# Attention and mixture kernel on one core: softmax sums divided out of the attention output, zero-padded rows in the third score term, one step order

## The chip, the core and the metric

The kernel runs on one core of a Trainium2 chip. The core has five engines with instruction queues of their own: TensorE (PE; its weight loads are shown apart as PEld), VectorE (DVE), ScalarE (ACT), GpSimd (POOL) and SyncE (SP), which here issues every DMA. Engines meet only at semaphores. The metric is device time in microseconds (us) for one launch; lower is better. Three runs of the kernel before took 892.65, 895.05 and 895.09 us, a median of 895.05 us.

## The reference

Three layers run in a row, all results in float32.

```
q, k, v: 4 batches, 12 heads, 448 rows, head size 64
rmsnorm(x, g) = x / sqrt(mean(x*x) + 1e-6) * g
attn = softmax(rmsnorm(q, g_q) @ rmsnorm(k, g_k).T / 8)      # e / (sum(e) + 1e-9)
x = heads side by side of attn @ v                           # 1792 x 768
g = x @ w_gate;  val = x @ w_val                             # 768 x 1536 each
h = g * sigmoid(g) * val;   x2 = h @ w_out                   # 1536 x 768
logits = x2 @ phi                                            # 32 slots, 4 for each of 8 experts
dispatch = softmax over tokens, combine = softmax over slots
slot_out[e] = relu((dispatch.T @ x2)[e] @ w1[e]) @ w2[e]     # 768 -> 1024 -> 768
out = combine @ slot_out                                     # 1792 x 768
```

w_gate, w_val and w_out arrive as float64 words.

## The kernel before

**Steps.** Two heads of one batch are a pair; there are 24 pairs, six a batch. A pair has four blocks of 112 queries, so c = 0 to 3 counts the steps of a pair, and `t` counts the 96 attention steps. From step 28 on each step also does one unit `u` of 128 columns of gate or value (`gv`, L573): 18 matmuls in two halves, G0 and G1. Even units are gate, odd ones value; 24 units make a batch, 96 make all four. A step of one batch's gate and value therefore goes beside the attention of the batch that follows.

**Order.** All of it stands in `tc.manual_schedule()`: each engine executes its instructions in the order in which the Python code issues them. A step is a dictionary of small functions, and a list of their names says in which order they are called. `ORD0` (L1200) is for steps 0 to 27 (`step0`), `ORD1` for the first batch's gate and value, `ORD2` for the next two batches, `ORD3` for the last.

**Attention of a pair.** q and k are squared (ACT), summed (DVE), turned into inverse roots (POOL, L336 and L337) and multiplied in (POOL, L343). PE transposes them (T, L368). Each is then split into a high part (TH, ACT) and a low part (L, DVE), since a product in the fast float32 format keeps fewer bits; a score is high*high + high*low + low*high. From pair 7 on a stationary tile `qa` holds, for one head, 64 rows of high parts and 64 of low parts of q, and `ka` two copies of k's high parts, so one 128-row matmul gives two terms (L458). The third term, q high by k low (`kl`), is a matmul of 64 rows for each head (L460). Then per head: row maximum (M0, M1; DVE, L465), exponential with its row sum (E0, E1; ACT, L473).

**Dividing by the sums.** `normp` (L478) adds 1e-9 to the two sums of a step (L483), takes reciprocals (L485) and multiplies both heads' 112x448 probabilities in place (L493), all on DVE, one step later. After that PE transposes the probabilities (P0, P1, L503; two steps behind the scores), and V0, V1 (L517) copy them out of PSUM. `pv` (X, L531) multiplies with v; `pv_evac` splits the result into high and low parts `xh`, `xl` for gate and value.

**Weights.** A block of float64 words is made float32 in three moves: two `w_relu` (POOL, L197, R), which give a positive part `hpos` and a negative part `hneg`; `w_top` (POOL, L203), which subtracts one from the other; `w_conv` (DVE, L208, C), which adds the low bits. There is one `hneg` buffer and two `hpos` buffers. Twelve blocks of w_out come in steps 0 to 23, twenty-four of gate and value beside the first batch; later batches read the float32 copy back from DRAM. Each unit's weight is split by `w_hi` (ACT, WH) and `w_lo` (DVE, WL, L235).

**PSUM.** One tag of three buffers (`pt_tile`, L67) serves all transposes, `xp`, the slot logits and the rest in turn; the scores have banks of their own.

**After the steps.** The last part streams the experts' weights from HBM, as buffers come free.

Of the kernel before, what the change touches and what calls it, by code (L numbers as in the profile page):

```python
# [21 lines left out]
def attn_moe_softmoe_kernel(  # L22
# [15 lines left out]
    nc = tc.nc  # L38
# [15 lines left out]
    PRB, PTB = 6, 2  # L54
# [24 lines left out]
    early = tc.alloc_tile_pool(name="early", bufs=1, side="left")  # up to the last batch  # L79
# [90 lines left out]
    def w_load(u):  # L170
        """w_out block u - or, from NO on, gate / value block u - NO."""
# [14 lines left out]
    def w_relu(u, js=(0, 1)):  # L186
        hp, hn = hset[u % 2]
        top = wst[u]["r64"][:, 4 : 4 + 4 * DM].rearrange("p (n w) -> p n w", w=4)[:, :, 0]
        for j in js:
# [5 lines left out]
            else:  # L195
                # what is below zero becomes zero as it is written
# [26 lines left out]
    def w_hi(u):  # L223
        # the last batch has two of them, and its low parts take the place of what they come from
# [13 lines left out]
    def wp_trans(f, hf):  # L238
        """half of w_out block f, transposed."""
# [12 lines left out]
    def wp_mul(f):  # L252
        """w_out @ phi with the slots on the partitions, as sums over four groups of rows of phi."""
# [29 lines left out]
    def load(i, what):  # L283
# [9 lines left out]
        else:  # L293
            vt = ap_.tile([CP, 2, NC, HD], F32, tag="vt", name="vt", bufs=3)
# [8 lines left out]
    def norm_sq(i, ns=(0, 1)):  # L303
        """squares of q and k."""
# [25 lines left out]
    def norm_rs(i, ns=(0, 1)):  # L330
        """one over the root of the mean squares."""
# [7 lines left out]
    def norm_mul(i, n, eng):  # L339
        """q or k over the root of its rows' mean squares, pairs of heads side by side."""  # L340
# [34 lines left out]

    def qk_tiles(i):
        d = st[i]
        if "qa" not in d:
            d["qa"] = ap_.tile([P, 2, S], F32R, tag="qa", name="qa", bufs=2)
            d["ka"] = ap_.tile([P, 2, S], F32R, tag="ka", name="ka", bufs=2)  # L380
            d["kl"] = ap_.tile([P, S], F32R, tag="kl", name="kl", bufs=2)
# [22 lines left out]
    def transp_lo(i, n):  # L404
        """low parts: of q beside the high parts of its head, under a second copy of which k's high parts are."""
# [4 lines left out]
        if i < SPL:  # L410
# [9 lines left out]
            else:  # L420
                sub_lo(kl, tq[:, :S], ka[:, 0])
            return
        for j, r in enumerate(halves):
# [10 lines left out]
            else:  # L434
                sub_lo(kl[r], tq[r, :S], ka[r, j])
# [4 lines left out]
    def scores(t):  # L440
        """scores of a block of queries of two heads; PE."""
# [10 lines left out]
        if i < SPL:  # L452
            for n, (wt, mv) in enumerate(((qa[:, 0], ka[:, 0]), (qa[:, 0], kl), (qa[:, 1], ka[:, 0]))):
# [7 lines left out]
        d[c] = {"sc": sc, "sm": ap_.tile([CP, 4], F32, tag="sm", name="sm", bufs=4), "pr": {}}  # L461

    def smax(t, j):
        d = st[t // NC][t % NC]
        nc.vector.tensor_reduce(  # L465
            out=d["sm"][:, 2 + j : 3 + j], in_=d["sc"][j], axis=AX.X, op=ALU.max, negate=True
        )

    def sexp(t, j):
        d = st[t // NC][t % NC]  # L470
        sm = d["sm"]
        p = ap_.tile([CP, S], F32, tag="pr", name="pr", bufs=PRB)
        nc.scalar.activation(  # L473
            out=p, in_=d["sc"][j], func=AF.Exp, bias=sm[:, 2 + j : 3 + j], accum_out=sm[:, j : j + 1]
# [3 lines left out]
    def normp(t, part=None):  # L478
        """probabilities over their sums."""
        d = st[t // NC][t % NC]  # L480
        pr, sm = d["pr"], d["sm"]
        if part in (0, None):
            nc.vector.tensor_scalar(out=sm[:, :2], in0=sm[:, :2], scalar1=EPS_SUM, scalar2=None, op0=ALU.add)  # L483
        if part in (1, None):
            nc.vector.reciprocal(out=sm[:, :2], in_=sm[:, :2])  # L485
        for j in range(2):
            if part in (2 + j, None):
                if (NP0 if t < M0 else NP1)[t % 2][j] == "p":
                    nc.gpsimd.tensor_scalar(
                        out=pr[j], in0=pr[j], scalar1=sm[:, j : j + 1], scalar2=1.0, op0=ALU.mult, op1=ALU.mult  # L490
                    )
                else:
# [934 lines left out]
```

## Time and profile before

| | us |
|---|---|
| median of three runs | 895.05 (892.65 to 895.09) |
| profiled execution, first to last instruction | 891.2 |
| PE busy | 813.3 (91%) |
| DVE busy | 615.8 (69%) |
| ACT busy | 469.1 (53%) |
| POOL busy | 329.0 (37%) |

The page gives the profiled execution as its span of 891.2 us; the runs' times are 1.4 to 3.9 us above that. Busy shares over the whole span mix parts of different kinds, so the rows below are read by stretches. An idle time is put down to the instruction whose end released it. A float32 matmul of attention output (`xp`) counts as two instructions in the trace.

### The profile page before, as it was taken

Reading aid. Unit: us, or ns where it says so; the run is one execution under the profiler, and the core shown is the slowest. Engines: PE = TensorE matmul, PEld = TensorE weight load, DVE = VectorE, ACT = ScalarE, POOL = GpSimd, SP = SyncE. Lnnn points to the kernel's source line nnn. Section 1 sums busy time; section 2 is a strip of 40 time slices with the busy share of each in tenths; the row PEclk is TensorE's granted clock in tenths of the full one; section 3 lists DMA queues with packets and bytes.
Section 4 is the critical chain, followed back from the end, with each engine's and each line's share of the span. In section 5 each row is a group of like instructions: output and inputs, shape, how many; then the busy total and the mean of one; then the engine's idle time right before and its main releaser. Section 6 shows DMA issues by size and latency. Waiting matters only on the chain.

```text
span 891.2 us, 14391 instructions
## 1 busy us (share of the span) xinstructions
PE 813.3 (91%) x5464; PEld 591.6 (66%) x5464; DVE 615.8 (69%) x1073; ACT 469.1 (53%) x1005; POOL 329.0 (37%) x234
## 2 busy tenths in 40 slices
PE   6888976988988999999999999999999999988675
PEld 6544544766766667777778767787787888745343
DVE  5999999999999996777777777776534443321012
ACT  4767765465556566666667656765532333311012
POOL 8997788877877932032211322120000000001000
PEclk9999999899999999999999999999999999999988
DMA  6645355545645442222232212221214887899997
GB/s 214 191 139 180 114 183 180 168 145 175 189 146 165 141 156 85 82 78 64 86 102 85 77 62 85 64 82 56 65 41 159 284 292 284 326 333 404 402 358 239
DMA packets 77891, 148.87 MB, mean 167 GB/s; under 512 B 5888, under 2 KB 48128, under 8 KB 77824
## 3 DMA queue, kind: packets, MB, share of 16 engines
q1 hardware_dynamic: 77824, 147.97, 50.4%
q8 instruction: 43, 0.70, 0.3%
q14 instruction: 24, 0.20, 0.1%
HBM read 128.29 MB, written 19.66 MB: 166 GB/s over the span
## 4 chain that ended last, share of the span: by engine, by line
PE 61%; DVE 26%; DMA 8%; issue 3%; ACT 1%; POOL 1%; SPq 0%; ACTq 0%; POOLq 0%; DVEq 0%
PE pg L584 33%; DVE pr L493 6%; DMA w<-in_moe_w_dram 5%; PE tp L503 5%; PE xp L531 5%; DVE sm L465 4%; DVE sm L483 4%; DVE raw L208 3%; PE s L458 2%; PE s L460 2%; PE th L619 2%; DVE wl L235 2%; PE lp L640 1%; PE sp L707 1%; DVE ss L323 1%
## 5 line engine op out<-in xcount | busy, mean ns | idle before, releaser
L584 PE MATMUL pg<-xh,wh 128*128 128x448 f32 x576 | 226.7, 394 | 0.0
L584 PE MATMUL pg<-xl,wh 128*128 128x448 f32 x576 | 212.3, 369 | 0.0
L473 ACT ACTIVATE pr<-s,sm 112x448 f32<-112x448 f32 x192 | 121.7, 636 | 91.3 <-DVE sm L465 87.7
L584 PE MATMUL pg<-xh,wl 128*128 128x448 f32 x432 | 159.7, 370 | 0.0
L465 DVE TENSOR_REDUCE sm<-s 112x1 f32<-112x448 f32 x192 | 116.3, 617 | 39.1 <-PE s L460 36.4
L517 ACT COPY pt<-tp 112x448 f32<-112x448 f32 x185 | 98.8, 534 | 74.6 <-PE tp L503 72.8
L493 DVE TENSOR_SCALAR pr<-pr,sm 112x448 f32<-112x448 f32 x192 | 133.3, 716 | 1.4
L503 PE MATMUL tp<-ident,pr 112*112 112x112 f32 x768 | 110.3, 269 | 23.7 <-DVE pr L493 15.3
L584 PEld LDWEIGHTS pg<-xh,wh 128*128 128x128 f32 x576 | 110.0, 191 | 21.5 <-issue 14.1
L503 PEld LDWEIGHTS tp<-ident,pr 112*112 112x112 f32 x768 | 82.0, 137 | 62.4 <-issue 19.6
L584 PEld LDWEIGHTS pg<-xl,wh 128*128 128x128 f32 x576 | 110.2, 191 | 6.5
L336 POOL TENSOR_SCALAR ss<-ss 112x16 f32<-112x16 f32 (+1 forms) x25 | 15.2, 608 | 245.7 <-DVE ss L323 232.0
L227 ACT CAST wh<-raw 128x768 fp32r<-128x768 f32 x96 | 79.8, 832 | 35.9 <-PE pg L584 29.3
L584 PEld LDWEIGHTS pg<-xh,wl 128*128 128x128 f32 x432 | 82.6, 191 | 7.0
L203 POOL TENSOR_TENSOR hpos<-hpos,hneg 128x768 f32<-128x768 f32 x36 | 78.4, 2177 | 3.0
L337 POOL TENSOR_TENSOR ri<-ss,mhalf 112x16 f32<-112x16 f32 (+1 forms) x25 | 72.1, 2884 | 2.1
L235 DVE TENSOR_TENSOR wl<-raw,wh 128x768 fp32r<-128x768 f32 x70 | 69.2, 988 | 0.7
L483 DVE TENSOR_SCALAR sm<-sm 112x2 f32<-112x2 f32 x96 | 53.2, 555 | 11.6 <-ACT pr L473 11.6
L599 DVE SCALAR_TENSOR_TENSOR ht<-ht,pg 128x448 f32<-128x448 f32 x48 | 29.5, 615 | 42.8 <-ACT ht L598 42.7
L531 PE MATMUL xp<-pt,vt 112*64 112x448 f32 x288 | 58.1, 545 | 0.0
L197 POOL TENSOR_SCALAR hneg<-r 128x768 uint16<-128x768 uint16 x36 | 54.5, 1514 | 2.7
L343 POOL TENSOR_TENSOR qn<-qk,ri 112x512 f32<-112x512 f32 x46 | 53.2, 1167 | 1.3
(155 smaller groups left out, 1181.2 us busy)
## 6 DMA issues: line engine op xcount, KB each, us to landing
w<-in_moe_w_dram SPq DMA_DIRECT2D x25, 1536.0 KB, 10.3
raw<-w SPq DMA_DIRECT2D x72, 384.0 KB, 3.2
w<-raw SPq DMA_DIRECT2D x36, 384.0 KB, 5.7
r<-in_moe_w_out_dram SPq DMA_DIRECT2D x12, 768.0 KB, 5.5
r<-in_moe_w_gate_dram SPq DMA_DIRECT2D x12, 768.0 KB, 5.2
r<-in_moe_w_val_dram SPq DMA_DIRECT2D x12, 768.0 KB, 5.2
qk<-in_q_dram SPq DMA_DIRECT2D x24, 224.0 KB, 4.2
qk<-in_k_dram SPq DMA_DIRECT2D x24, 224.0 KB, 4.7
```

The source lines that it names most:

```text
L203: nc.gpsimd.tensor_tensor(out=hp, in0=hp, in1=hn, op=ALU.subtract)
L227: (nc.vector.tensor_copy if u - NO < NU and WH1 == "v" else nc.scalar.copy)(out=wh, in_=wst[u]["raw"])
L235: eng.tensor_tensor(out=wl, in0=wst[u]["raw"], in1=wst[u]["wh"].bitcast(F32), op=ALU.subtract)
L337: nc.gpsimd.tensor_tensor(out=ri, in0=ss, in1=mhalf[:, : len(ns)], op=ALU.pow)
L465: nc.vector.tensor_reduce(out=d["sm"][:, 2 + j : 3 + j], in_=d["sc"][j], axis=AX.X, op=ALU.max, negate=True)
L473: nc.scalar.activation(out=p, in_=d["sc"][j], func=AF.Exp, bias=sm[:, 2 + j : 3 + j], accum_out=sm[:, j : j + 1])
L483: nc.vector.tensor_scalar(out=sm[:, :2], in0=sm[:, :2], scalar1=EPS_SUM, scalar2=None, op0=ALU.add)
L493: nc.vector.tensor_scalar(out=pr[j], in0=pr[j], scalar1=sm[:, j : j + 1], scalar2=None, op0=ALU.mult)
L503: nc.tensor.transpose(tp[:CP, ck * CP : (ck + 1) * CP], pr[:, ck * CP : (ck + 1) * CP], ident[:CP, :CP])
L517: eng(out=st[i]["pt"][j][:, :, c * CP : (c + 1) * CP], in_=st[i][c]["tp", j][:CP, :S].rearrange("p (k q) -> p k q", k=NC),)
L531: nc.tensor.matmul(xp[HD * j : HD * j + HD, :S], d["vt"][:, j, ck, :], d["pt"][j][:, ck, :], start=(ck == 0), stop=(ck == NC - 1),)
L584: nc.tensor.matmul(d[r], wt[:, P * c : P * c + P], mv, start=(c == 0 and n == 0), stop=(c == KD - 1 and n == 2),)
```

## The change

The probabilities are no longer divided. The eight row sums of a pair (four steps, two heads) are kept in `su`. Once a pair, `sums_inv` (NA) adds 1e-9 on ACT, takes the reciprocals on DVE and spreads them on POOL to 112 x 512; `sums_spread` (NB) transposes that with four PE transposes into a PSUM tile `rb`; `sums_evac` (NC) copies it to SBUF on ACT; `pv_scale` (XM) multiplies the attention output in PSUM by it on DVE. High and low parts are then made from the SBUF result. The transposes of the probabilities follow the scores by one step instead of two, with four instead of six buffers for them, and v has two buffers instead of three.

The third score term of the pairs from 7 on becomes a matmul over all 128 rows: `kl` is one of two fixed tiles whose other halves are zeroed at the start. For w_out blocks and value units `w_top` moves from POOL to DVE, into `w_conv`. In steps 0 to 27 every second head's probabilities are copied out by DVE instead of one in eight. The tanh of the gate and its multiplication are separate items (AT, AM). q and k of pair i+3 are loaded at c = 0 instead of c = 2, the squares at c = 3 instead of the next c = 0; those of pair 2 stand ahead of step 0. One list, `ORD1`, gives the step order for all batches.

```diff
-    PRB, PTB = 6, 2
+    PRB, PTB = 4, 2
...
-    def w_top(u):
+    def w_top(u, eng):
         hp, hn = hset[u % 2]
-        nc.gpsimd.tensor_tensor(out=hp, in0=hp, in1=hn, op=ALU.subtract)
+        eng.tensor_tensor(out=hp, in0=hp, in1=hn, op=ALU.subtract)
+
+    def top_late(u):
+
+        return u < NO or (u - NO) % 2
 
     def w_conv(u):
+        if top_late(u):
+            w_top(u, nc.vector)
...
-            vt = ap_.tile([CP, 2, NC, HD], F32, tag="vt", name="vt", bufs=3)
+            vt = ap_.tile([CP, 2, NC, HD], F32, tag="vt", name="vt", bufs=2)
...
     def norm_part(i, c):
-        if c == 0:
-            norm_sq(i)
+        if c == 3:
+            norm_sq(i + 1)
         elif c == 1:
             norm_rs(i)
-        else:
+        if c >= 2:
             norm_mul(i, c - 2, nc.gpsimd)
...
+    klz = [ap_.tile([P, 2, S], F32R, name=f"kl{n}") for n in range(2)]
+
+    def kl_zeros():
+        for n in range(2):
+            for j, r in enumerate(halves):
+                nc.gpsimd.memset(klz[n].bitcast(F32)[halves[1 - j], j], 0.0)
...
-                sub_lo(kl[r], tq[r, :S], ka[r, j])
+                sub_lo(kl[r, j], tq[r, :S], ka[r, j])
...
             for j in range(2):
                 nc.tensor.matmul(sc[j], qa[:, j, cs], ka[:, j], start=True, stop=False)
-            for j, r in enumerate(halves):
-                nc.tensor.matmul(sc[j], qa[r, j, cs], kl[r], start=False, stop=True)
+            for j in range(2):
+                nc.tensor.matmul(sc[j], qa[:, j, cs], kl[:, j], start=False, stop=True)
...
-    def normp(t, part=None):
-        """probabilities over their sums."""
...
+    def sums_inv(i):
+
+        su = st[i]["su"].rearrange("p c j -> p (c j)")
+        nc.scalar.activation(out=su, in_=su, func=AF.Copy, bias=EPS_SUM)
+        nc.vector.reciprocal(out=su, in_=su)
+        rs = ap_.tile([P, 2 * NC * HD], F32, tag="rs", name="rs", bufs=1)
+        nc.gpsimd.tensor_copy(
+            out=rs[:CP].rearrange("p (n d) -> p n d", d=HD), in_=su.unsqueeze(2).to_broadcast([CP, 2 * NC, HD])
+        )
+        st[i]["rs"] = rs
+
+    def sums_spread(i):
+
+        rs = st[i]["rs"][:CP].rearrange("p (c n) -> p c n", c=NC)
+        rb = pt_tile("rb")
+        for c in range(NC):
+            nc.tensor.transpose(
+                rb[:, c * CP : (c + 1) * CP], rs[:, c], ident[:CP, :CP]
+            )
+        st[i]["rb"] = rb
+
+    def sums_evac(i):
+        st[i]["rs"] = st[i]["rs"][:, :S]
+        nc.scalar.copy(out=st[i]["rs"], in_=st[i].pop("rb")[:, :S])
...
-    def pv_evac(i):
+    def pv_scale(i):
+
         b, hp = pairs[i]
-        xt[b, hp] = st.pop(i)["xp"][:, :S]
+        d = st.pop(i)
         if b == 3 and hp > 3:
             xf = xfp.tile([P, S], F32, tag=f"xh{hp - 4}", name="xf", bufs=1)
-            nc.scalar.copy(out=xf, in_=xt[b, hp])
-            xt[b, hp] = xf
         else:
-            split(b, hp)
+            xf = d["rs"]
+        nc.vector.tensor_tensor(out=xf, in0=d["xp"][:, :S], in1=d["rs"], op=ALU.mult)
+        xt[b, hp] = xf
...
         def P_(j):
-            if t - 2 < NT_ and (t > M0 or PLAG == 2):
-                ptrans(t - 2, j)
+            if t - 1 < NT_:
+                ptrans(t - 1, j)
...
-        if c == 2:
+        if c == 0:
             load(i + 3, "qk")
...
     ORD1 = (
-        "NA T NB S ND P1 X Z3 SS A XV P0 Q W4 M0 TH WH M1 Z1 R L Z2 Z4 WL V0 G0 NC C E0 E1 SP HT G1 "
-        "LG V1"
-    ).split()
-    ORD2 = (
-        "NA R SP NB X P0 A W4 T S WH TH V0 M0 NC XV C E0 Z3 G0 ND L Z4 P1 Z1 SS V1 M1 E1 HT G1 Z2 Q "
-        "WL LG"
-    ).split()
-    ORD3 = (
...
+        "AT NB X NC T S XM TH XH M0 M1 AM XL E0 E1 SP W4 G0 L NA Z1 Z3 WH P0 V0 P1 V1 Z2 Z4 HT LG SS C WL G1 R Q"
     ).split()
...
-    PVD = [(2, 1)]
+    PVD = [(n, 1) for n in range(4)]
...
         load(1, "qk")
         setup()
+        kl_zeros()
         fill(16)
...
         scores(0)
+        norm_sq(2)
         for t in range(NT_ + 4):
```

The next rows are VectorE's queue from the row maxima of a step with c = 0 on, beside the first batch's gate and value (`qa` is q's low part, `ss` the sum of squares, `wl` the low weights, `ht` gate or value, `hpos` and `raw` the weight conversion). Before:

```order
L465 TENSOR_REDUCE sm<-s 112x1 x2
L426 SCALAR_TENSOR_TENSOR qa<-tq,gsc,qa 64x448 x2
L235 TENSOR_TENSOR wl<-raw,wh 128x768
L493 TENSOR_SCALAR pr<-pr,sm 112x448
L208 SCALAR_TENSOR_TENSOR raw<-r_3357,hpos_107 128x768
L483 TENSOR_SCALAR sm<-sm 112x2
L485 RECIPROCAL sm<-sm 112x2
L493 TENSOR_SCALAR pr<-pr,sm 112x448
L323 TENSOR_REDUCE ss<-qn 112x16
L599 SCALAR_TENSOR_TENSOR ht<-ht,pg 128x448
```

The same step after the change:

```order
L478 TENSOR_REDUCE sm<-s 112x1 x2
L639 SCALAR_TENSOR_TENSOR ht<-ht,pg 128x448
L439 SCALAR_TENSOR_TENSOR qa<-tq,gsc,qa 64x448 x2
L497 RECIPROCAL su<-su 112x8
L679 TENSOR_TENSOR lg<-lp,lg 128x448
L329 TENSOR_REDUCE ss<-qn 112x16
L203 TENSOR_TENSOR hpos_107<-hpos_107,hneg 128x768
L214 SCALAR_TENSOR_TENSOR raw<-r_3015,hpos_107 128x768
L241 TENSOR_TENSOR wl<-raw,wh 128x768
```

The four rows L493, L483 and L485 are gone, one reciprocal of a pair (L497) and one subtraction (L203) have come, and `ht` now stands ahead of `qa`. (`lg`, the slot logits, comes once in eight steps in either kernel.)

On PE, beside the gate and value of later batches, the step in which `xp` is made (`pg` are gate and value products, `tp` probabilities, `tq` q or k, `s` scores). Before:

```order
L584 MATMUL pg<-xh,wl 128x448
L531 MATMUL xp<-pt,vt 64x448 x8
L503 MATMUL tp<-ident,pr 112x112 x4
L458 MATMUL s<-ka,qa 112x448 x2
L460 MATMUL s<-kl,qa 112x448 x2
L584 MATMUL pg<-xh,wh 128x448
```

After:

```order
L612 MATMUL pg<-xh,wl 128x448
L509 MATMUL rb<-ident,rs 128x112 x4
L552 MATMUL xp<-pt,vt 64x448 x8
L374 MATMUL tq<-ident,qn 128x112 x4
L471 MATMUL s<-ka,qa 112x448 x2
L473 MATMUL s<-kl_110,qa 112x448 x2
L612 MATMUL pg<-xh,wh 128x448
```

Four transposes `rb` have come ahead of `xp`, the two of L473 now use all rows, and `tp` has moved behind the first half of gate or value.

On ACT at the very start (`qn` 112x1024 are the squares of pair 2, `qa` is q of pair 1, `pr` the first step's exponentials). Before:

```order
L394 CAST ka<-tq 128x448
L392 ACTIVATE qa<-tq,gsc 128x448
L473 ACTIVATE pr,sm<-s,sm 112x448 x2
L313 ACTIVATE qn<-qk 112x1024
L394 CAST ka<-tq 128x448
```

After:

```order
L407 CAST ka<-tq 128x448
L319 ACTIVATE qn<-qk 112x1024
L405 ACTIVATE qa<-tq,gsc 128x448
L488 ACTIVATE pr,su<-s,sm 112x448 x2
L407 CAST ka<-tq 128x448
```

The squares of pair 2, which need a DMA, have moved ahead of the first exponentials.

## Rows read from the trace of the kernel before

**Rows 1.** Busy time of the engines by stretch, TensorE's granted clock, DMA.
```profile
14.00:146.00 132.00, 105.45 (x798) 62.22 (x795) 128.81 (x228) 92.19 (x228) 111.50 (x82) 0.95 0.55 166
146.00:339.00 193.00, 172.13 (x925) 129.46 (x925) 186.77 (x261) 109.44 (x234) 143.96 (x87) 0.96 0.51 159
339.00:655.00 316.00, 316.00 (x1834) 238.19 (x1835) 225.29 (x447) 206.34 (x433) 57.20 (x36) 1.00 0.25 76
655.00:771.00 116.00, 116.00 (x604) 96.14 (x600) 47.41 (x67) 35.94 (x56) 0.29 (x1) 1.00 0.66 234
771.00:892.00 121.00, 92.04 (x1165) 54.54 (x1164) 22.09 (x61) 20.08 (x48) 5.02 (x13) 0.92 0.94 344
```
**Rows 2.** DVE by line, 14 to 146 us: count, busy us, mean ns, idle before.
```profile
L493 DVE TENSOR_SCALAR pr<-pr,sm 112x448 f32<-112x448 f32 x54 | 42.8, 815 | 0.6
L483 DVE TENSOR_SCALAR sm<-sm 112x2 f32<-112x2 f32 x28 | 20.4, 728 | 0.0
L517 DVE COPY pt<-tp 112x448 f32<-112x448 f32 x6 | 3.7, 611 | 0.0
```
**Rows 3.** DVE by line, 146 to 339 us.
```profile
L493 DVE TENSOR_SCALAR pr<-pr,sm 112x448 f32<-112x448 f32 x48 | 49.6, 1033 | 0.8
L465 DVE TENSOR_REDUCE sm<-s 112x1 f32<-112x448 f32 x49 | 28.1, 614 | 0.9 <-PE s L460 0.9
L483 DVE TENSOR_SCALAR sm<-sm 112x2 f32<-112x2 f32 x25 | 26.8, 1072 | 0.0
L235 DVE TENSOR_TENSOR wl<-raw,wh 128x768 fp32r<-128x768 f32 x24 | 24.2, 1008 | 0.3
L426 DVE SCALAR_TENSOR_TENSOR qa<-tq,gsc,qa 64x448 fp32r<-64x448 f32 x12 | 8.2, 684 | 0.3
L606 DVE SCALAR_TENSOR_TENSOR ht<-ht,pg 128x448 f32<-128x448 f32 x12 | 7.4, 615 | 1.7 <-PE pg L584 1.5
```
**Rows 4.** The same for 339 to 655 us: one line of DVE.
```profile
L483 DVE TENSOR_SCALAR sm<-sm 112x2 f32<-112x2 f32 x44 | 7.3, 166 | 11.6 <-ACT pr L473 11.6
```
**Rows 5.** POOL by line, 146 to 339 us.
```profile
L203 POOL TENSOR_TENSOR hpos<-hpos,hneg 128x768 f32<-128x768 f32 x21 | 48.4, 2304 | 1.8
```
**Rows 6.** L531 on PE, 146 to 339 us: durations, first and last start.
```profile
L531 PE MATMUL xp<-pt,vt x96: 539/539/590, 165.0 to 326.8; 112*64 112x448 f32 x96
```
**Rows 7.** Chain of waits, three times the `xp` block: start us, us.
```profile
436.18 3.16 PE xp L531 x16
...
463.83 3.16 PE xp L531 x16
...
490.44 3.16 PE xp L531 x16
```
**Rows 8.** PE in order of time, one step of the second batch's gate and value: start us, us.
```profile
439.27 0.59 PE L503 MATMUL tp<-ident,pr 112*112 112x112 f32 x4
439.63 0.64 PE L458 MATMUL s<-ka,qa 128*112 128x448 f32 x2
440.20 0.46 PE L460 MATMUL s<-kl,qa 64*112 64x448 f32 x2
440.59 0.47 PE L584 MATMUL pg<-xh,wh 128*128 128x448 f32 x1
440.90 0.36 PE L584 MATMUL pg<-xl,wh 128*128 128x448 f32 x1
441.10 0.36 PE L584 MATMUL pg<-xh,wl 128*128 128x448 f32 x1
```
**Rows 9.** PE in order of time, three steps of the first part.
```profile
97.60 0.86 PE L503 MATMUL tp<-ident,pr 112*112 112x112 f32 x4 [1.71 <-DVE pr L493]
...
102.36 0.55 PE L243 MATMUL tw<-ident,raw 128*128 128x128 f32 x3
...
106.05 0.55 PE L243 MATMUL tw<-ident,raw 128*128 128x128 f32 x3
```
**Rows 10.** ACT in order of time, the start.
```profile
15.84 0.63 ACT L473 ACTIVATE pr<-s,sm 112x448 f32<-112x448 f32 x1
...
18.21 1.06 ACT L313 ACTIVATE qn<-qk 112x1024 f32<-112x1024 f32 x1 [1.03 <-DMA qk<-in_k_dram]
```

More of the change, by code (lines that the diff above doesn't have):

```diff
@@ L465, in smax @@
         nc.vector.tensor_reduce(
[L466 removed]
+            out=d["sm"][:, j : j + 1], in_=d["sc"][j], axis=AX.X, op=ALU.max, negate=True
         )
     def sexp(t, j):
[L470 to L471 removed]
+        i, c = divmod(t, NC)
+        d = st[i][c]
+        if "su" not in st[i]:
+            st[i]["su"] = ap_.tile([CP, NC, 2], F32, tag="su", name="su", bufs=3)
         p = ap_.tile([CP, S], F32, tag="pr", name="pr", bufs=PRB)
@@ L473, in sexp @@
         nc.scalar.activation(
-            out=p, in_=d["sc"][j], func=AF.Exp, bias=sm[:, 2 + j : 3 + j], accum_out=sm[:, j : j + 1]
+            out=p, in_=d["sc"][j], func=AF.Exp, bias=d["sm"][:, j : j + 1], accum_out=st[i]["su"][:, c, j : j + 1]
         )
         d["pr"][j] = p
-    def normp(t, part=None):
[L480 to L492, printed above, removed]
-                    nc.vector.tensor_scalar(
-                        out=pr[j], in0=pr[j], scalar1=sm[:, j : j + 1], scalar2=None, op0=ALU.mult
-                    )
+    def sums_inv(i):
[7 more added lines that the diff above has]
+        st[i]["rs"] = rs
@@ L564, in attn_moe_softmoe_kernel, with split_hi, split_lo, now @@
     pools_x = []
-    def split(b, c):
-        xh, xl = x_tiles(b, c)
-        src = xt.pop((b, c))
-        evac_hi(xh, src)
-        sub_lo(xl, src, xh)
-        xs[b, c] = (xh, xl)
+    def split_hi(b, c):
+        xs[b, c] = x_tiles(b, c)
+        evac_hi(xs[b, c][0], xt[b, c])
+    def split_lo(b, c):
+        xh, xl = xs[b, c]
+        sub_lo(xl, xt.pop((b, c)), xh)
+    def now(i):
+        b, hp = pairs[i]
+        return b < B - 1 or hp <= 3
     def gv(u, part):
@@ L899, in M_, with NA, NB, NC_ @@
             smax(t, j)
-        def N_(part):
-            if t >= NLAG:
-                normp(t - NLAG, part)
+        def NA():
+            if ip >= 0 and cp == 0:
+                sums_inv(ip)
+        def NB():
+            if ip >= 0 and cp == 1:
+                sums_spread(ip)
+        def NC_():
+            if ip >= 0 and cp == 1:
+                sums_evac(ip)
         def C_():
@@ L946, in R_ @@
                 w_relu(f, (1,))
-                w_top(f)
             if r == 1 and f + 1 < NO:
@@ L975, in X_, with xv, XM, XH @@
                 pv(ip, [cp])
-        def XV():
-            if ip >= 0 and (cp == NC - 1 or (ip == NP - 1 and cp == 1)):
-                pv_evac(ip)
+        def xv():
+            return ip >= 0 and (cp == NC - 1 or (ip == NP - 1 and cp == 1))
+        def XM():
+            if xv():
+                pv_scale(ip)
+        def XH():
+            if xv():
+                split_hi(*pairs[ip])
+        def XL():
+            if xv():
+                split_lo(*pairs[ip])
         def G4():
@@ L983, in G4 @@
                 w_relu(wu(u + 4))
-                w_top(wu(u + 4))
+                if not top_late(wu(u + 4)):
+                    w_top(wu(u + 4), nc.gpsimd)
         def G2():
@@ L1008, in step0 @@
             w_store(wu(u + 2))
-        if c == 2:
+        if c == 0:
             load(i + 3, "qk")
-        if c == 1:
+        if c == 1 and i > 0:
+            load(i, "v")
+        if t == M0 - 1:
             load(i + 1, "v")
@@ L1030, in step, with NA, NB, NC_ @@
         nxt = c < 2 and i + 1 < NPR
-        def N_(part):
-            if t - 1 < NT_ and (t > M0 or NLAG == 1):
-                normp(t - 1, part)
-        def A_():
+        def NA():
+            if c == 0 and NP < i <= NPR:
+                sums_inv(i - 1)
+        def NB():
+            if c == 1 and NP < i <= NPR:
+                sums_spread(i - 1)
+        def NC_():
+            if c == 1 and NP < i <= NPR:
+                sums_evac(i - 1)
+        def AT():
+            if prev is not None and prev % 2 == 0:
+                act_gate(prev)
+        def AM():
             if prev is not None:
-                (act_val if prev % 2 else act_gate)(prev)
+                (act_val if prev % 2 else act_gate_mul)(prev)
         def W4():
@@ L1061, in X_, with XM, XH, XL @@
         def X_():
-            if c == 2 and NP < i <= NPR:
+            if c == 1 and NP < i <= NPR:
                 pv(i - 1, range(NC))
-        def XV():
-            if c == 2 and NP < i <= NPR:
-                pv_evac(i - 1)
+        def XM():
+            if c == 1 and NP < i <= NPR:
+                pv_scale(i - 1)
+        def XH():
+            if c == 1 and NP < i <= NPR and now(i - 1):
+                split_hi(*pairs[i - 1])
+        def XL():
+            if c == 1 and NP < i <= NPR and now(i - 1):
+                split_lo(*pairs[i - 1])
         def Z1():
@@ L1125, in R_ @@
                 w_relu(wu(u + 4))
-                w_top(wu(u + 4))
+                if not top_late(wu(u + 4)):
+                    w_top(wu(u + 4), nc.gpsimd)
         def C_():
@@ L1156, in step @@
         )
-        order = ORD1 if u < NU else ORD2 if u < last else ORD3
-        for n in order:
+        for n in ORD1:
             items[n]()
```

48 lines of the change are left out of this document (24 added, 24 removed).

## The prediction

> **What bounds the kernel now.** I read the table of engines by stretch first [rows 1], then VectorE (DVE) line by line in two of its stretches, then TensorE (PE) in order of time. The table is to show that the limit changes. From 14 to 146 us (A: the 28 attention steps before gate and value begin) DVE is busy 128.8 of 132 us; from 146 to 339 (C: 24 steps, first batch's gate and value) 186.8 of 193. From 339 to 655 (D: the next 48 steps but for a little) PE is busy 316.0 of 316 and DVE 225. From 655 to 771 (E, last batch) PE is busy throughout again. Behind that the DMA share is 0.94 while the experts' weights stream in. So DVE work is worth time in A and C, PE work in D and E.
>
> The lines of DVE say what fills it. The multiplication of the probabilities, L493, takes 42.8 us in A and 49.6 in C; the addition of 1e-9 to two numbers, L483, takes 20.4 and 26.8 [rows 2, 3]. L483 moves nothing: in D the same instruction takes 166 ns [rows 4], in C 1072 ns. POOL is busy 144 of 193 us in C and 57 of 316 in D [rows 1], so most of L483's time, and part of L493's, is time in which DVE stands behind POOL. It goes with the instruction.
>
> The length of a step comes from the attention output `xp`, one block a pair. In C its first and last instruction start at 165.0 and 326.8; that is six blocks, and the last instruction of a block starts some 3.0 us after its first, so a pair takes (326.8 - 3.0 - 165.0) / 5 = 31.8 us, 7.94 a step [rows 6]. In D two pairs follow each other in 27.65 and 26.61 us, 27.13 on average or 6.78 a step, with PE never idle [rows 7]. The same PE work thus takes 1.16 us a step longer in C.
>
> **The change part by part.** DVE in A: L493 and L483 go, -63.2 us. There come 12 subtractions `w_top` for w_out and about one for a value unit. The trace has no such subtraction on DVE; the nearest row is L235, the same size and two operands in SBUF, 1008 ns [rows 3], and the upper bound is POOL's own 2304 ns [rows 5]. I take L235, which is the same engine: 13 us. 28 - 6 = 22 copies of probabilities at 611 ns [rows 2] are 13.4, six multiplications of the output at about the same 0.61 are 3.7. DVE falls by 33 to 96 us, 3.4 a step against 4.7. What is late next is PE: a step in which it barely waits takes 106.05 - 102.36 = 3.69 us, while in others it stands, 1.71 us behind L493 in one place [rows 9]. The four transposes `rb` cost 0.36 us a pair, as `tp` does (439.27 to 439.63) [rows 8], so PE's floor is 3.8 a step, 106 us. ACT (92 of 132 us) gives away copies and gets few, so PE, ACT and DVE then lie within 0.8 us a step of each other, in fixed order and chained through three PSUM buffers. I do not expect the floor but a step half-way, 4.2 us: -14. The bounds are -26 (the floor) and 0.
>
> Against that stands the start. The squares of pair 2 now stand ahead of the first exponentials on ACT, and they begin only at 18.21, when their DMA has landed; the first exponentials began at 15.84 [rows 10]. Behind them on ACT wait q of pair 1 and all of step 0. They end at 19.3, so step 0 is late by 3.4 us, of which some is regained since DVE waited for the same sums later anyway: +2.5. A in all: -11.5.
>
> DVE in C: L493 and L483 go, -76.4; 12 subtractions (12 us) and six multiplications (4) come. 186.8 becomes 126, 5.3 a step, below PE's 6.8. POOL, the other candidate, had 144 us and loses 12 subtractions of 2.3 [rows 5]; 116 plus six spreads of a microsecond or so stays near 5.1 a step. So C falls to PE's pace in D plus what the change does to PE there.
>
> PE, a pair in C and D. The three-term scores take 0.96 us (439.63 to 440.59) and the first gate or value matmul after them 0.31, where the next takes 0.20 (440.90 to 441.10) [rows 8]. So switching to the two 64-row matmuls and back costs something: first L458, two matmuls, lasts 0.57 until L460 starts. Four matmuls of one kind at 0.20 and no switch would be 0.8 to 0.9 for the scores and 0.2 for the one after them: 0.2 us less a step, 0.8 a pair. `rb` adds 0.36. One wait comes: with c = 0 the transposes of h need the PSUM buffer that q's low part (two `qa`) reads last. From the end of the scores DVE needs 2 * 0.614 + 0.615 + 2 * 0.684 = 3.2 us to be through [rows 3]; PE gets there after nine products and two `tp`, 9 * 0.20 + 2 * 0.36 = 2.5 [rows 8]. That is about 0.6 us, and what is queued behind on PE is all of G1. Sum +0.16 a pair, between -0.44 (no wait) and +1 (twice the wait and half the saving).
>
> The Trainium skill, page "TensorEngine Tiling (Array Packing)", has two rules on this. "Theoretical Speedup" promises up to 2x for 64-row matmuls side by side, which speaks against padding: the third term would cost a matmul more a step. "Key Properties" says that changing the tiling mode drains the engine; the 0.57 and 0.31 of [rows 8] agree with that. By the first rule alone the result is the third rival below; by the second it is the forecast.
>
> So C: 24 steps at 6.78 + 0.04 are 163.7 us, -29.3; its first units still come out of A's conversion queue on POOL, for which I leave 2.8: -26.5, with bounds -31 and -12. D: 12 pairs at +0.16, +2, with bounds -5 and +12. E and what follows: no instruction is added or taken, the slot logits only move ahead of G1; 0.
>
> At nothing I cost: the probabilities' buffers (four hold two steps, and their transposes now come in the next step); the second v buffer (its reader runs two steps ahead of the load); the earlier q and k load, behind which on SP wait the weight blocks, which have two steps before POOL needs them; tanh apart from its product; the four memsets of `kl` on POOL, which has nothing to do until the first sums arrive; and the chain of `rb`, whose sums are complete in the step before c = 0 ends: reciprocal behind `qa`, spread on POOL, some 4.6 us after the scores, while PE comes to it after about 5.3. That cover is the thinnest; without it each pair loses what is missing.
>
> Sum: -11.5 - 26.5 + 2 = -36 us. From the profiled span of 891.2 that is 855; the runs lie 1.4 to 3.9 us above it, and from their median of 895.05 it is 859.
>
> **The rivals.** First, more: A reaches 3.9 a step (-20), C and D run without the wait at the transposes of h (-31 and -5). Sum -56, 839 us. For it: DVE is at 97% in A and C with waits behind POOL in its own busy time, and a faster PE keeps its clock (0.95 and 0.96 granted there against 1.00 in D). Against: the in-order chain.
>
> Second, less: the engines that come next in A eat the gain (-3), and in C DVE, POOL and PE hold each other up at 7.4 a step (-15); D +3. 880 us. For it: POOL at 75% in C, the shared `hneg` buffer now goes back and forth between POOL and DVE. Against: DVE's 5.3 and POOL's 5.1 leave 1.5 us a step.
>
> Third, padding costs what packing saved: a matmul more instead of 0.2 less, 0.4 us a step in the 68 steps of pairs 7 to 23, +27: 886 us. Against it: 0.96 us for what would be 0.8 in four equal matmuls [rows 8].
>
> Fourth, slower: `rb`. PE is in order, and `rb` stands ahead of `xp`. If POOL's spread lands late, because it waits for DVE's reciprocal and then behind weight conversion, PE stands once in each of 17 pairs from step 28 on. It decides from 36 / 17 = 2.1 us a pair; at 3 us it is 859 + 51 = 910 us. For it: POOL's load in C. Against: in D POOL has 57 us of work in 316, so there it cannot last.
>
> **How the numbers follow.** Forecast 0.55, first rival 0.2, second 0.14, third 0.06, fourth 0.05. A measurement of this kernel tells about 0.3%, 2.7 us, from no change. Faster holds for the first three and nearly all of the third rival: 0.94; within 0.3%: 0.02; slower: 0.04. The range takes in the first and the second rival, 836 to 883 us, and leaves half of the others out.
>
> **What the changed profile would show.** Right: DVE in C at about two thirds of the stretch, POOL's remaining lines shorter, PE at 95% or more of C, `xp` blocks 27 to 28 us apart there as in D; scores block of L471 and L473 with starts 0.20 apart and no longer first matmul behind it. A wait of half a microsecond at the transposes of h with c = 0. Wrong: PE idle behind POOL's spread at `rb`, steps in C above 7.4 us, scores blocks of 1.1 us, or `xp` blocks in D 29 us apart. The sum fails if A does not fall below 125 us, or if D moves by more than 10.

## The result, and the profile after

The changed kernel takes 873.88 us (median of 4 runs, 869.46 to 874.62), the kernel before beside it 894.58: a ratio of 0.977, 95% interval 0.974 to 0.980, so 20.7 us less. The forecast was 859, inside a range of 836 to 883; the measured time is nearer to the second rival's 880. The profiled execution took 874.62 us with a span of 872.5.

The table of engines by stretch comes first, as [rows 1], with the borders of A and C moved to the same work (the first gate and value product of the first and of the 25th unit) and the later ones moved by the same 28 us.

```profile
core 0: us, PE busy (x) PEld busy (x) DVE busy (x) ACT busy (x) POOL busy (x), PEclk, DMA share, GB/s
14.00:141.00 127.00, 108.78 (x826) 66.08 (x824) 100.65 (x162) 83.64 (x217) 84.70 (x71) 0.95 0.56 165
141.00:311.00 170.00, 161.50 (x947) 132.54 (x946) 148.73 (x187) 113.00 (x248) 132.37 (x86) 1.00 0.59 185
311.00:627.00 316.00, 309.25 (x1834) 249.72 (x1833) 180.18 (x290) 202.69 (x449) 63.82 (x48) 1.00 0.24 74
627.00:743.00 116.00, 115.62 (x611) 97.50 (x610) 48.18 (x68) 37.13 (x59) 1.16 (x2) 1.00 0.63 222
743.00:872.00 129.00, 98.50 (x1204) 61.15 (x1203) 24.52 (x65) 21.58 (x51) 5.01 (x13) 0.95 0.93 340
```

A is now 127 us long (132 before), C 170 (193). In C TensorE is busy 95% and VectorE 87%; in D TensorE is no longer busy throughout, 309 of 316. By the starts of the first products, the same work in both kernels: A lost 5.7 us (146.4 to 140.7), C 21.7 (192.4 to 170.7 for 24 units), while D grew by 7.3 (306.9 to 314.2 for the 44 units, 11 pairs, from the 25th to the 69th). What follows grew by 1.4.

VectorE's lines in C, against [rows 3]:

```profile
L241 DVE TENSOR_TENSOR wl<-raw,wh 128x768 fp32r<-128x768 f32 x24 | 35.0, 1458 | 2.2 <-ACT wh L233 2.2
L214 DVE SCALAR_TENSOR_TENSOR raw<-r,hpos 128x768 uint32<-128x768 uint32 x22 | 28.3, 1288 | 3.5 <-POOL hpos L203 2.7
L478 DVE TENSOR_REDUCE sm<-s 112x1 f32<-112x448 f32 x48 | 27.6, 616 | 5.5 <-PE s L473 5.1
L203 DVE TENSOR_TENSOR hpos<-hpos,hneg 128x768 f32<-128x768 f32 x11 | 10.4, 949 | 0.0
```

The addition and the multiplication are gone, and `w_top` costs 949 ns, where 1008 was taken. But the same low part of the weights, L241 here and L235 before, went from 1008 to 1458 ns: VectorE still stands behind POOL, at other instructions.

TensorE in D, against [rows 8] (columns: start, us from first start to last end, engine, line, operation and tile, count, idle before and what ended it):

```profile
421.24 0.36 PE L612 MATMUL pg<-xh,wl 128*128 128x448 f32 x1
421.44 0.57 PE L471 MATMUL s<-ka,qa 128*112 128x448 f32 x2
421.84 0.57 PE L473 MATMUL s<-kl,qa 128*112 128x448 f32 x2
422.25 0.36 PE L612 MATMUL pg<-xh,wh 128*128 128x448 f32 x1
422.46 0.37 PE L612 MATMUL pg<-xl,wh 128*128 128x448 f32 x1
...
429.70 0.93 PE L524 MATMUL tp<-ident,pr 112*112 112x112 f32 x8
431.11 0.62 PE L652 MATMUL th<-ident,ht 128*112 128x128 f32 x4 [0.48 <-DVE qa L439]
```

Four score matmuls now take 0.81 us (421.44 to 422.25) where they took 0.96, and the product behind them 0.21 where it took 0.31. The transposes of h wait for q's low part, as forecast: 1.41 us after `tp` began, where `tp` takes 0.7 (424.08 to 424.78 where nothing waits).

### The profile page after: what moved, and what is told of

It reads as the page before. It is cut to its first block, busy times and chain, and to the rows that moved or that the text cites. A ratio compares the mean times of both kernels' runs of the same rounds, so it can differ in the third digit from the quotient of the medians.

```text
span 872.5 us, 14355 instructions
## 1 busy us (share of the span) xinstructions
PE 805.2 (92%) x5560; PEld 618.0 (71%) x5560; DVE 507.7 (58%) x782; ACT 463.2 (53%) x1030; POOL 299.7 (34%) x238
## 4 chain that ended last, share of the span: by engine, by line
PE 67%; DVE 12%; DMA 9%; POOL 5%; ACT 3%; issue 2%; SPq 0%; POOLq 0%; ACTq 0%; DVEq 0%
PE pg L612 32%; PE tp L524 6%; PE xp L552 6%; DMA w<-in_moe_w_dram 6%; DVE sm L478 3%; PE s L471 3%; PE s L473 2%; PE th L652 2%; DVE qa L439 2%; PE s L468 2%; PE tq L374 2%; POOL rs L499 2%; PE lp L673 1%; ACT pr L488 1%; PE s L552 1%
## 5 line engine op out<-in xcount | busy, mean ns | idle before, releaser
L612 PE MATMUL pg<-xh,wh 128*128 128x448 f32 x576 | 217.8, 378 | 0.0
L478 DVE TENSOR_REDUCE sm<-s 112x1 f32<-112x448 f32 x192 | 110.7, 615 | 60.3 <-PE s L473 57.7
L499 POOL COPY rs<-su 112x512 f32<-112x512 f32 x24 | 27.5, 1147 | 291.2 <-DVE su L497 291.1
L524 PE MATMUL tp<-ident,pr 112*112 112x112 f32 x768 | 98.1, 265 | 18.2 <-ACT pr L488 8.3
L241 DVE TENSOR_TENSOR wl<-raw,wh 128x768 fp32r<-128x768 f32 x70 | 78.9, 1127 | 25.7 <-ACT wh L233 25.4
L538 ACT COPY pt<-tp 112x448 f32<-112x448 f32 x164 | 81.4, 543 | 17.0 <-PE s L552 8.6
L626 ACT ACTIVATE ht<-pg 128x448 f32<-128x448 f32 x48 | 26.2, 546 | 67.0 <-PE pg L612 67.0
L612 PE MATMUL pg<-xh,raw 128*128 128x448 f32 x144 | 52.7, 366 | 0.0
L653 ACT COPY hn<-th 112x512 f32<-112x512 f32 x48 | 28.6, 596 | 44.1 <-PE th L652 42.1
L349 POOL TENSOR_TENSOR qn<-qk,ri 112x512 f32<-112x512 f32 x46 | 50.3, 1104 | 2.1
```

What stands on the lines that cost most here:

```text
L241: eng.tensor_tensor(out=wl, in0=wst[u]["raw"], in1=wst[u]["wh"].bitcast(F32), op=ALU.subtract)
L349: eng.tensor_tensor(out=st[i]["qn"][:, n].rearrange("p c h d -> p h c d"), in0=st[i]["qk"][:, n], in1=st[i]["ri"][:, n] .rearrange("p (h c ...
L478: nc.vector.tensor_reduce(out=d["sm"][:, j : j + 1], in_=d["sc"][j], axis=AX.X, op=ALU.max, negate=True)
L499: nc.gpsimd.tensor_copy(out=rs[:CP].rearrange("p (n d) -> p n d", d=HD), in_=su.unsqueeze(2).to_broadcast([CP, 2 * NC, HD]))
L524: nc.tensor.transpose(tp[:CP, ck * CP : (ck + 1) * CP], pr[:, ck * CP : (ck + 1) * CP], ident[:CP, :CP])
L538: eng(out=st[i]["pt"][j][:, :, c * CP : (c + 1) * CP], in_=st[i][c]["tp", j][:CP, :S].rearrange("p (k q) -> p k q", k=NC),)
```

## The experiments

All are compared with the kernel before on the same chip (892.95 to 895.84 us). The last four columns are read from the profiled runs: the start of the first product of the first, third, 25th and 69th unit of gate and value, in us.

| kernel | us | ratio, 95% interval | 1st | 3rd | 25th | 69th |
|---|---|---|---|---|---|---|
| before | 894.58 | 1 | 146.4 | 168.5 | 338.8 | 645.7 |
| changed | 873.88 | 0.977 (0.974 to 0.980) | 140.7 | 160.4 | 311.4 | 625.6 |
| pad_alone | 888.01 | 0.992 (0.990 to 0.994) | 148.9 | 170.6 | 341.1 | 640.5 |
| packed | 884.62 | 0.989 (0.986 to 0.991) | 139.5 | 159.4 | 314.1 | 636.2 |
| no_eps | 873.16 | 0.975 (0.973 to 0.978) | 143.9 | 161.1 | 318.1 | 625.0 |
| eps_tt | 894.81 | 0.999 (0.997 to 1.001) | 148.3 | 170.9 | 341.4 | 649.0 |
| pad_eps_act | 863.59 | 0.967 (0.963 to 0.970) | 145.6 | 162.2 | 318.1 | 617.5 |
| x_early | 870.43 | 0.973 (0.970 to 0.975) | 142.2 | 157.6 | 308.3 | 622.4 |
| x_early_g2 | 874.10 | 0.977 (0.975 to 0.978) | 142.9 | 160.1 | 310.6 | 624.7 |
| top_pool | 882.21 | 0.985 (0.983 to 0.988) | 147.0 | 167.2 | 322.3 | 636.5 |
| ht_late | 868.75 | 0.971 (0.969 to 0.974) | 138.9 | 158.6 | 309.7 | 619.7 |
| ht_late_na | 858.36 | 0.959 (0.957 to 0.961) | 139.6 | 159.3 | 304.2 | 610.3 |
| both | 856.84 | 0.958 (0.956 to 0.959) | 140.2 | 157.4 | 302.4 | 608.5 |
| hybrid | 852.42 | 0.955 (0.952 to 0.959) | 140.4 | 158.4 | 303.4 | 606.5 |

In A packed, ht_late and ht_late_na run the changed kernel's instructions; their first units start between 138.9 and 140.7. Differences of 2 us in A say nothing. TensorE's granted clock in A (the mean share of full speed) goes with them: 0.99 in ht_late, 0.97 in packed, 0.96 in ht_late_na, 0.95 in the changed kernel. It is 0.95 in the kernel before, but 0.92 in no_eps, 0.90 in pad_eps_act and eps_tt, 0.89 in pad_alone and 0.87 in top_pool, so what these say of A is blurred by it. From 14 us to the first unit, in ht_late and in top_pool:

```profile
14.00:138.85 124.85, 104.60 (x824) 63.64 (x825) 103.25 (x162) 83.88 (x217) 85.93 (x71) 0.99 0.56 168
14.00:147.04 133.04, 116.39 (x824) 69.96 (x823) 92.27 (x151) 83.06 (x217) 108.55 (x86) 0.87 0.53 164
```

### The third score term

packed: `qa[:, j, cs], kl[:, j]` back to `qa[r, j, cs], kl[r, j]`. pad_alone: the same edit the other way in the kernel before, with `klz` and its zeros, and v loaded later.

> The changed kernel with the third score term of pairs 7 to 23 as before: two matmuls over 64 rows each, side by side, instead of two over 128 rows with zeros. Theory (switching between 64-row pairs and full rows costs more than the packing saves, 0.21 us a step): stage D 0.84 us a pair slower, 10 us over its 12 pairs, 12 to 14 us in all, about 887 us. Rival (the block was short in the changed kernel for another reason, such as the clock or the order): no slower than 875; by the packing's gain alone it would be faster, 874 - 27 = 847 us.

> The kernel before with the padded third term alone (zeroed tiles, full rows; to make room, five buffers of probabilities instead of six, two of v instead of three). Theory: stage D is bound by TensorE and gets 0.8 us a pair shorter, 10 us; stage C is bound by VectorE and gets nothing; stage A nothing. In all -8 to -12 us, 0.990 of before. Rival (C gains too, since the score blocks stand in its chain): -14 us. Rival (padding costs): +20 us or more.

Against the changed kernel packed lost 7.9 us in D (322.1 for 314.2 between the 25th and the 69th unit), 0.72 a pair, and 3.8 in C between the third and the 25th (154.8 for 150.9). pad_alone gained 7.5 in D, 0.68 a pair, and nothing in C (170.5 for 170.3), where VectorE sets the pace. Both sides agree: two full-row matmuls with zeros cost less here than two 64-row matmuls side by side. That the change between the two kinds is what costs was not tried by itself; the time is lost at the matmuls next to the packed ones (L471 and the products, +8.7 us in D). The third rival falls. The Trainium skill, "TensorEngine Tiling (Array Packing)", "Theoretical Speedup", gives up to 2x for a small dimension of 64 or less; no such gain is seen in this place.

### The small addition

no_eps leaves out L483 (the division is by the bare sums):

```
-            nc.vector.tensor_scalar(out=sm[:, :2], in0=sm[:, :2], scalar1=EPS_SUM, ...)
+            pass
```

eps_tt puts `nc.vector.tensor_tensor(out=sm[:, :2], in0=sm[:, :2], in1=epst, op=ALU.add)` in its place. pad_eps_act is pad_alone with `nc.scalar.activation(out=sm[:, :2], in_=sm[:, :2], func=AF.Copy, bias=EPS_SUM)` there.

> The kernel before without the addition of 1e-9 to the sums (L483), everything else as it was; the sums are divided by as they are. Theory of the prediction (L483 is VectorE standing behind POOL, and the time goes with the instruction): stages A and C are bound by VectorE and lose most of its 20.4 and 26.8 us, -25 to -40 in all, about 862 us. Rival (what VectorE waits for there is still held when the next instruction, the reciprocal L485, comes, which then takes the millisecond's worth of waits over): L485 grows from 0.17 to about a microsecond in C, and the kernel gets 0 to 8 us shorter, 890 us.

> The kernel before with the addition of 1e-9 to the sums (L483) done with a second operand, a tile of 1e-9, instead of a constant: TENSOR_TENSOR with two inputs in SBUF in place of TENSOR_SCALAR, at the same place and of the same two elements. First theory (only a TENSOR_SCALAR or copy between SBUF tiles has to wait until POOL's instruction is through; the two-input L208 took 937 to 1086 ns in all of A and C of the kernel before and the reciprocal 165 to 167): the addition takes about 0.2 us, and the kernel is as fast as without it, 873 us. Second theory (an instruction with two inputs in SBUF waits for POOL as well, and L208 was spared only because the addition and L493 had waited already): it takes about a microsecond in C again, 890 to 896 us.

> The kernel of pad_alone (kernel before, padded third term) with the addition of 1e-9 to the sums on ScalarE, two elements a step; the probabilities are still multiplied, L493, and the order of the steps is that of before. Theory (the two small edits give their gains in different stages, -22 for the addition in A and C, -8 for the padding in D): 865 us, so less than the whole change's 874. Rival (the division of the output is what frees stage C: with L493 left, C does not reach TensorE's pace, and padding adds nothing there): 872 us or more.

Without this one instruction a step the kernel before is as fast as the whole change makes it (873.2 and 873.9 us), though 862 was expected. The steps from the third to the 25th unit shrink from 170.3 to 157.0 us, the two units ahead from 22.1 to 17.2 (the granted clock there was 0.79 before and 0.93 in no_eps), A by 2.5. The time did not go with the instruction in full, though. VectorE's lines from 146 to 306 us, in no_eps:

```profile
L493 DVE TENSOR_SCALAR pr<-pr,sm 112x448 f32<-112x448 f32 x44 | 50.8, 1155 | 0.8
L235 DVE TENSOR_TENSOR wl<-raw,wh 128x768 fp32r<-128x768 f32 x22 | 27.3, 1242 | 0.3
L485 DVE RECIPROCAL sm<-sm 112x2 f32<-112x2 f32 x22 | 3.4, 152 | 0.0
```

The reciprocal did not take the wait over: 20 of its 22 began while a POOL instruction was under way, and all took 149 to 156 ns. L235 did in part: 1242 ns, 1008 in [rows 3]. A step lost 0.60 us (13.3 / 22) of the addition's 1.07; of the other 0.47, L235 accounts for about 0.2.

In eps_tt the addition with two operands waited just as long. Its durations (min/median/max, ns) in C, and one place in order of time:

```profile
L485 DVE TENSOR_TENSOR sm<-sm,epst x25: 149/948/1809, 148.2 to 338.1; 112x2 f32<-112x2 f32 x25
```

```profile
140.45 2.07 POOL L345 TENSOR_TENSOR qn<-qk,ri 112x512 f32<-112x512 f32 x1
...
142.07 2.23 DVE L485 TENSOR_TENSOR sm<-sm,epst 112x2 f32<-112x2 f32 x1
142.48 1.81 POOL L237 TENSOR_TENSOR wl<-raw,wh 128x768 fp32r<-128x768 f32 x1
...
144.76 0.15 DVE L487 RECIPROCAL sm<-sm 112x2 f32<-112x2 f32 x1
144.94 0.73 DVE L495 TENSOR_SCALAR pr<-pr,sm 112x448 f32<-112x448 f32 x1
```

Two elements take 2.23 us: they begin under one POOL instruction and end at 144.30, when the next, a subtraction, ends (144.29). So the second theory holds. The Trainium skill says this in "SBUF — State Buffer", "SBUF: two separate sides": a VectorE instruction in a two-port mode, or one with two SBUF inputs against a POOL instruction that reads SBUF, shares one lock with POOL, and the loser waits for the whole instruction. The trace agrees, down to two elements.

pad_eps_act needs only the padding, with the smaller buffers that make room for it, and the addition on ScalarE, where it takes 0.22 us (median). It is faster than the whole change (0.967 of before, 0.963 to 0.970, for 0.977, 0.974 to 0.980): the two gains add, as expected (865).

### Stage A

x_early: in `step0`, `divmod(t - NC - 2, NC)` becomes `divmod(t - NC - 1, NC)`, and the conditions for the last pair follow. x_early_g2 has in addition `X XM XH XL G2 G3 G4` at the end of `ORD0`. top_pool: `top_late` returns False, and the relu of w_out is followed by `w_top(f, nc.gpsimd)`.

> The changed kernel with the attention output of a pair (X, and with it the sums' reciprocal, the spread, the scaling and the split) one step earlier in the steps up to 27. Theory (a ring of buffers holds stage A): probabilities are now transposed one step after their exponentials, but a pair's two transposed tiles take the place of those of the pair before last, which xp reads last in that same step, so once in eight steps ScalarE stands some 2.6 us at the copy L538 behind TensorE. With xp a step earlier the copy finds its tile free: the waits of L538 behind L552 go, stage A gets 5 to 8 us shorter, the kernel 0.6 to 0.9% faster than the changed kernel, about 867 us. Rival (the step of stage A is a chain through all engines in which this wait is only where the slack shows): stage A stays within 2 us of what it was, 874 us.

> The kernel of x_early with the split of the next weight block (G2) ahead of the conversion of the blocks after it (G3, G4), and the output's scaling and split ahead of all three, in the steps up to 27. Theory (the first gate and value units wait for POOL's and VectorE's queues, in which the conversion of later blocks stands ahead of what the next unit needs): the first product starts 2 to 4 us earlier than in x_early and the third unit as much, 867 us. Rival (POOL has that much work at the change of stages in any order): the third unit starts within 1 us of x_early, 870 us.

> The changed kernel with all subtractions of the weight conversion (w_top) on POOL again, as before. Theory (VectorE is no longer the bound in A and C, POOL has room in A but less in C): A within 2 us, since the chain of stage A stands in the ring of transposed tiles; C 3 to 6 us slower by 12 subtractions of 2.3 us on POOL; 878 us. Rival (the subtraction on VectorE, just ahead of the conversion it feeds, is what holds the steps of A): A 4 to 8 us shorter, 868 us.

The place in the changed kernel: ScalarE's copy of transposed probabilities waits for `xp`, and TensorE for ScalarE.

```profile
90.01 0.97 PE L552 MATMUL s<-pt,vt 112*64 112x448 f32 x4
...
91.01 0.53 ACT L538 COPY pt<-tp 112x448 f32<-112x448 f32 x1 [2.63 <-PE s L552]
...
92.84 0.60 PE L524 MATMUL tp<-ident,pr 112*112 112x112 f32 x4 [1.38 <-ACT pr L488]
```

The first and last row maximum of the same 16 steps, in the changed kernel and in x_early:

```profile
L478 DVE TENSOR_REDUCE sm<-s x33: 570/611/618, 46.5 to 120.6; 112x1 f32<-112x448 f32 x33
```

```profile
L478 DVE TENSOR_REDUCE sm<-s x33: 570/612/617, 47.6 to 117.3; 112x1 f32<-112x448 f32 x33
```

A step took 4.65 us before (46.0 to 120.4), 4.63 after ((120.6 - 46.5) / 16), 4.36 with `xp` a step earlier. The wait at L538 (5.3 us in these steps) is gone there, so the ring is the likely cause of most of the 0.27 us a step. A rival remains: the granted clock in these steps was 1.00 in x_early and 0.95 in the changed kernel, and TensorE's busy time 64.7 us for 65.6. At the third unit 1 to 3 us of this are left, since the last four steps take it back. x_early_g2 did not mend that: its third unit starts 2.5 us later than x_early's. What holds the change of stages is open. top_pool made A 6.3 us and the steps from the third to the 25th unit 4.2 us longer: the subtractions on VectorE pay (0.985 of before, 0.983 to 0.988, for 0.977), and its rival falls. Its theory had C right but not A, of which it expected nothing; how much of the 6.3 is the lower clock (0.87 for 0.95) is open.

### Stages C and D

ht_late moves `HT LG` behind `G1` in `ORD1`; ht_late_na also moves `NA` to the second place. both is ht_late_na with x_early. hybrid is both with `SW = 13`: from pair 13 on the probabilities are multiplied on VectorE again.

> The changed kernel with the transposes of h (HT) and the slot logits (LG) behind the second half of gate and value (G1) in the steps from 28 on. Theory (the wait of the forecast: TensorE stands 0.6 us a pair at L652 until q's low part, L439 on VectorE, has read the PSUM buffer): nine products of 0.2 us now cover it, the wait at L652 goes, and stages C and D get 0.64 us a pair shorter, 17 pairs, -8 to -11 us, about 864 us. Rival (VectorE's lateness comes back at the next instruction that waits for it, as the next step's transposes need the same PSUM buffers): no change, 874 us.

> The kernel of ht_late (transposes of h behind G1) with the sums' addition, reciprocal and spread (NA) moved from behind q's low part to the front of the step with c = 0. In ht_late the wait at L652 was gone, 7.6 us in stage D, but the time behind L652 had grown by 3.5 us, with TensorE waiting at rb L509 for POOL's spread, 0.8 us at most. Theory (the thin cover named in the prediction: rb is now the first thing of the next step and the spread comes too late): with the sums ready a microsecond or two earlier the wait at rb goes and D loses 3 to 4 us more, 865 us. Rival (rb waits for something else that comes last by a little, such as its PSUM buffer): same as ht_late within 1 us, 869 us.

> The edits of ht_late_na (transposes of h behind G1, sums' reciprocal and spread at the front) and of x_early (output of a pair one step earlier up to step 27) in one kernel. Theory (they act in different stages: stage A and the first units there, C and D here): the gains add, -2.8 us on the start of the third unit and -15 on the rest, about 855 us. Rival (the steps of stage C that start earlier wait for weights or POOL instead): 858 us or more, no gain over ht_late_na.

> The kernel of both edits (both), with the division as in the kernel before for pairs 13 to 23: sums, reciprocal and the two multiplications of the probabilities on VectorE at the front of the next step, no spread, no rb, the output split straight out of PSUM. Up to pair 12 the output is divided as in the changed kernel. Theory (dividing the output frees VectorE, which is worth time where VectorE waits behind POOL, in A and C, and costs TensorE four transposes a pair, 5.6 us of stage D, where VectorE has room): D goes from 306 to 300 us, that of pad_alone, the rest stays, 850 us. Rival (VectorE's longer line, 1.2 us a step, comes to stand in the path of the scores or of the transposes of h, as q's low part did): D 306 us or more, 857 or more.

The largest wait of TensorE between the 25th and the 69th unit, in the changed kernel and in ht_late (engine, line, what was waited for: us in total, times, longest):

```profile
PE th L652 <- DVE qa L439: 4.6, 10, 0.5
```

```profile
PE rb L509 <- POOL rs L499: 3.0, 4, 0.8
```

The one wait went, 7.6 us with what stood beside it, and half of that came back ahead of `rb`: D 310.0 for 314.2. With the sums earlier neither is left in the view, D is 306.1, and the steps from the third to the 25th unit take 144.9 us for 151.1, 6.59 each, with TensorE never idle. D's part, 3.9, is what was expected; C's 6.1 was not. The traces show where it lay: in C, too, ht_late freed 5.6 us behind `tp` and lost as much again, 4.3 behind the transposes of h, where `rb` waits up to 1.7 us, and 1.7 behind `xp`. both adds too little to tell from ht_late_na (its interval overlaps).

hybrid takes D to 303.1, half of what was expected. `rb` is gone (5.6 to 0.5 us, of the last divided pair), but `tp` and the transposes of h have 1.8 more behind them. Its whole time can't be told from both's. By its median it is the fastest of the kernels run.

## Why the prediction was right, and where it was off

The mechanism was right for C, the largest term: VectorE behind POOL set its pace (no_eps alone takes 13.3 us off its steps), and without it C fell nearly to TensorE's pace (146.9 us busy of 150.9 from the third to the 25th unit). For D the terms named were about right, but 3.0 us stood in none of them. For A it is not shown. The sum was -36 and came to -18.7 in the profiled spans, with all three terms short of the forecast; the range held it because it was made to hold the second rival too. Of the prediction's own signs, TensorE's 95% of C, the `xp` blocks there (27.2 to 28.5 us apart), the starts of the scores and the wait of 0.48 us came; VectorE at two thirds of C did not (87%), and A did not fall below 125 us, at which the prediction said that its sum fails.

- **A, -11.5, came to -5.7.** "I do not expect the floor but a step half-way, 4.2 us" failed twice. The floor of 3.8 rested on one short step of [rows 9], the kind without a product with phi. The step after it, with that product, takes 4.37 (106.05 to 110.42), and TensorE's busy time over 16 steps is 65.64 us in the changed kernel, 4.10 a step (4.03 before), so 4.2 was nearly the floor. And the steps kept their 4.6, probably in part because transposing one step earlier closed a ring: "At nothing I cost: the probabilities' buffers" counted the buffers ahead of the transposes, not the two tiles behind them. What was gained came in the last four steps (26.0 to 20.1 us up to the first unit). The start, +2.5, was 3.9 at the second step (row maxima at 16.58 and 20.45) but only 0.5 at the ninth. That VectorE's work set the length of A does not follow: its busy time there fell from 129 to 101 us and A by 5.7, and in top_pool it is 92 us while A is as long as before, though at a lower clock. Which edit gave the 5.7 us is open.
- **C, -26.5, came to -21.7.** The steps are as forecast, 6.86 us from the third to the 25th unit (150.9 / 22) for 6.82, but in part by luck. The 6.78 was read from two of the shorter pairs of D, where a step takes 6.97 over all 11 (306.9 / 44); C has less for TensorE than D, 6.59 a step where it never waits (ht_late_na), and in the changed kernel waits make up the rest. What failed is "2.8" for the first units: the first two take 19.8 us where 2 x 6.82 + 2.8 are 16.4 (22.1 before). The working of VectorE's load was off too (126 forecast, 148.7 measured), since waits behind POOL moved to L241 and L214, but it stayed below TensorE's 161.5. The spread on POOL, put at "a microsecond or so" without a row, took 0.61 us or 2.29, 1.45 on average. In the first unit TensorE stands for the low part that POOL makes, behind a subtraction of a later block:
```profile
139.87 1.84 POOL L203 TENSOR_TENSOR hpos<-hpos,hneg 128x768 f32<-128x768 f32 x1
141.66 1.80 POOL L241 TENSOR_TENSOR wl<-raw,wh 128x768 fp32r<-128x768 f32 x1
...
143.51 0.47 PE L612 MATMUL pg<-xh,wl 128*128 128x448 f32 x1 [2.26 <-POOL wl L241]
```

- **D, +2, came to +7.3.** TensorE's time from each start to the next, summed by line over the 11 pairs: products -4.6 and scores -4.8, so -0.85 a pair for the forecast -0.8. `tp` with the wait behind it +8.2, of which 7.6, 0.69 a pair, go in ht_late (forecast "about 0.6"; its own terms, 3.21 - 2.52, give 0.69); `rb` +5.5, 0.50 a pair (forecast 0.36, from `tp`; why these four cost more is open). What was not in the sum at all is 3.0: behind transposes of h +1.5, slot logits' sums +0.9, `tq` +0.6.
- **L483, "It goes with the instruction"**: a little over half of it did in C, as no_eps shows; of the rest, nearly half shows at the next instruction that needs the lock, L235.

The second rival saw A (-3) better than the forecast, but not C (7.4 a step). The fourth was there in small: `rb` waits once anything ahead of it gets shorter, at 0.8 us at most in D and 1.7 in C, less than the 2.1 a pair from which it decides. The first rival's time was out of reach of this order; with the wait at h and the one at `rb` removed the kernel still takes 858.

What the change holds beyond the padding and the addition, that is the division of the output, the subtractions on VectorE and the order, brought least. Against pad_eps_act it gives 1.8 us up to the third unit and 4.9 from there to the 25th (150.9 for 155.9) and costs 14.8 in D (314.2 for 299.4); mended as in ht_late_na it gives 3.0 and 10.9 and costs 6.7. The division of the output was not tried alone, and the subtractions are worth 4.2 of the 4.9 by top_pool.

## What to carry to other kernels

Where an instruction of two elements takes a microsecond, look at what another engine does in that time: moving that one instruction to ScalarE, where nothing held it, bought as much (0.992 to 0.967 of before) as the whole change did (0.977). A reordering that brings a producer a step earlier must be followed to every buffer behind it, not only to those ahead. And a floor is read from the busy time of an engine over several whole rounds, not from one short step.

## What the runs showed of the hardware

The wait of VectorE behind POOL is counted as VectorE's busy time, reaches instructions of two elements (eps_tt: median 948 ns in C, 160 in D where POOL is mostly idle), and passes in part to the next instruction of the kinds concerned when one is removed. The reciprocal of two numbers was never held: 149 to 156 ns in no_eps, mostly in the middle of a POOL instruction. The two-input L208 was hardly held in the kernel before (937 to 1086 ns in C). The same conversion, L214, took 957 to 960 ns in 12 of its 22 cases in C of the changed kernel, and 1245 to 2539 in the other ten, each of which began while a POOL instruction was under way and ended after it; five of the short ones began so too, but ended before it. The ten fit the second theory of eps_tt; the five show that not every one is held, and none of this was tried by itself. Two 64-row matmuls side by side between full-row ones cost 0.17 to 0.18 us a step more than two full ones with half of their rows zero (7.5 to 7.9 us over 44 steps).
